# A softmax's row sums in the spare columns of the score bank

## The chip, the core and the metric

The kernel runs on one core of a Trainium2 chip. The core has a matrix engine (TensorE, in the profile PE, with its weight loads as PEld), a vector engine (VectorE, DVE), an engine for functions (ScalarE, ACT), a general engine (GpSimd, POOL) and one that issues transfers (SyncE, SP). Each works through its own queue in order, and they wait for one another by semaphores. TensorE writes into PSUM, a small memory of eight banks with 512 fp32 columns on each of 128 partitions; SBUF is the large working memory. The metric is the time of one execution on the device, in microseconds.

## The reference

Three stages follow one another: sparse attention over 2 batches of 8 heads, 576 positions, 64 values a head; then four experts, each token weighting all of them; then a gated layer. What the change touches is the attention's softmax:

```
scores = scale * q @ k.T
mask_local   = (rel >= 0) & (rel < 32)                 # heads 0 to 3
mask_strided = (rel >= 0) & (pos_k % 32 == pos_q % 32) # heads 4 to 7
scores = where(mask, scores, -1e9)
scores = scores - max(scores, axis=-1)
attn = exp(scores)
attn = attn / (sum(attn, axis=-1) + 1e-09)
out = attn @ v
```

The result is turned to tokens by features and goes through the experts (`relu(x @ w1) @ w2`, weighted) and the gated layer (`sigmoid(x @ wg) * (x @ wv) @ wo`).

## The kernel before

The order of every engine's instructions is written out in the program; no scheduler changes it. A ledger in the program adds up assumed costs and decides from them where background work (conversion of weights) is put between the steps of the later stages.

The attention is cut into 32 groups, 16 in each batch. A group of the strided kind is a score tile of 72 rows by 4 blocks of 72 columns (288 columns), one of the local kind 96 rows by 3 blocks of 128 (384 columns); in each batch eight strided groups come first, then eight local ones. The first batch runs by itself at the start of the program (with small matmuls of zeros, `keep_warm`, in TensorE's pauses), the second is interleaved with the first products of the first expert. `attention` is a software pipeline: in step i the stages of `STAGES` run in the order values, transpose, scores, exp, norm, split, each on the group that it has come to:

- `pair_scores`, every other step, for two groups: two masks are written into two PSUM banks (line 717, tile `sps`), then the products of queries and keys are added to them (line 730). The pool of these banks has three of them; a bank is given to the next group when the instructions that used it are over.
- `group_exp`, for group i: VectorE takes the negated maximum of each block (`nm<-sps`), then ScalarE takes one exponential for each block (`P<-sps,nm`), with the maximum as bias. Each has an accumulator output: the sum over the block goes to one column of a small SBUF tile, `sm`. In the profile that output is a row of its own, ACTIVATION_READ_ACCUMULATOR, behind each ACTIVATE.
- `group_norm`, one step later: VectorE adds 1e-9 to the sums (TENSOR_SCALAR `sm<-sm`), takes the reciprocal, and GpSimd multiplies the exponentials by it in place (`P<-P,sm`).
- `group_transpose`, three steps behind: TensorE transposes the blocks into another bank (`tps`, line 756), VectorE copies them out (`PT`).
- `group_values`, `group_split`, five steps behind: the product with the values (line 780), and its split into a high and a low part (`xh`, `xl`) for the experts.

Around the groups the queries and keys are transposed by TensorE (`qkps`) and copied by ScalarE (`qsT`, `qlT`) and VectorE (`ksT`, `klT`), one pair of groups or more ahead; GpSimd and ScalarE split the weights of the first expert (`wh`, `wl`); the first expert's hidden values are evacuated by ScalarE (`hh`) and VectorE (`hl`). Helpers record these calls, so that all instructions of the three engines have line 101 in the profile, and tiles tell them apart.

Of the kernel before, what the change touches and what calls it, by code (L numbers as in the profile page):

```python
# [9 lines left out]
F32 = mybir.dt.float32  # L10
# [6 lines left out]
AF = mybir.ActivationFunctionType  # L17
ALU = mybir.AluOpType
# [88 lines left out]
def attn_moe_glu_kernel(ctx, tc, q, k, v, dp, w1, w2, wg, wv, wo, out):  # L107
    nc = tc.nc
    ledger = Ledger()
    dve, act, pool_ = (Reckoned(e_, name, ledger) for e_, name in ((nc.vector, "V"), (nc.scalar, "A"), (nc.gpsimd, "G")))  # L110
# [26 lines left out]
    atp = at_stack.enter_context(tc.tile_pool(name="atp", bufs=1, side="right", reuse_waits="tile"))  # L137
# [527 lines left out]
    pt_tiles, of_tiles, soft = {}, {}, {}  # L665
# [42 lines left out]
    def pair_scores(pair):  # L708


        tiles = []
        for kind, b, c, half, hh in pair:
            ps = sp_.tile([128, 512], F32, tag="s", name="sps")
            n, w, m = (NU, NU, 4) if kind == "s" else (96, 128, 3)
            pv_ = ps[:n, :m * w].rearrange("p (a b) -> p a b", b=w)
            mask = mask_s.unsqueeze(1).to_broadcast([NU, 4, NU]) if kind == "s" else mask_l[:, half:half + 3, :]
            nc.tensor.matmul(pv_, identb[:n, :n], mask, start=True, stop=False)  # L717
            soft[kind, b, c, half, hh] = (pv_, n, w, m)
            tiles.append(pv_)
        m = soft[pair[0]][3]  # L720
        for j in range(m):
            for pv_, (kind, b, c, half, hh) in zip(tiles, pair):
                if kind == "s":
                    lo = 64 * half
                    qs_, ks_ = QT["s", b, c, hh][lo:lo + 64, j, :], KT["s", b, c, hh][lo:lo + 64, j, :]
                else:
                    lo, i = 64 * c, 3 * half + j
                    q0, k0 = hh * S + 96 * i, hh * S + max(96 * i - 32, 0)
                    qs_, ks_ = QT["l", b][lo:lo + 64, q0:q0 + 96], KT["l", b][lo:lo + 64, k0:k0 + 128]
                nc.tensor.matmul(pv_[:, j, :], qs_, ks_, start=False, stop=j == m - 1)  # L730

    def group_exp(g):
        pv_, n, w, m = soft[g]
        nm = atp.tile([128, 4], F32, tag="nm", name="nm", bufs=4)
        sm = atp.tile([128, 4], F32, tag="sm", name="sm", bufs=4)
        pt = atp.tile([128, 384], F32, tag="P", name="P", bufs=3)
        pp = pt[:n, :m * w].rearrange("p (a b) -> p a b", b=w)
        dve.tensor_reduce(nm[:n, :m], pv_, AX.X, ALU.max, negate=True)
        for j in range(m):
            act.activation(  # L740
                pp[:, j, :], pv_[:, j, :], AF.Exp, bias=nm[:n, j:j + 1], accum_out=sm[:n, j:j + 1]
            )
        soft[g] = (pp, sm[:n, :m], n, w, m)

    def group_norm(g):
        pp, sm, n, w, m = soft[g]
        dve.tensor_scalar(sm, sm, 1e-9, None, ALU.add)
        dve.reciprocal(sm, sm)
        pool_.tensor_tensor(pp, pp, sm.unsqueeze(2).to_broadcast([n, m, w]), ALU.mult)

# [63 lines left out]
    def attention():  # L814

        gs = []
        for b in range(B):
            gs += [("s", b, c, half, hh) for c in range(2) for hh in range(2) for half in range(2)]
            gs += [("l", b, c, half, hh) for half in range(2) for hh in range(2) for c in range(2)]
        n = len(gs)  # L820
        stage = dict(values=group_values, transpose=group_transpose, scores=pair_scores,
                     exp=group_exp, norm=group_norm, split=group_split)

        def later(x):
# [564 lines left out]
```

## Time and profile before

| | us |
|---|---|
| median of the runs shown | 651.19 |
| lowest of them | 650.22 |
| the profiled execution | 651.06 |
| its span, first to last instruction | 648.9 |
| TensorE busy | 638.2 (98%) |
| VectorE busy | 440.3 (68%) |
| ScalarE busy | 341.7 (53%) |
| GpSimd busy | 265.5 (41%) |

The span is the profile's own; the 2.2 us between it and the execution's time lie ahead of the first and behind the last instruction. Times in a trace are counted from the start of the span. A busy TensorE is not one at its peak, since matmuls are pipelined and their ends are modelled. Idle time of an engine that nobody waits for costs nothing.

### The profile page before, as it was taken

What the parts mean: (1) busy time and instruction counts of PE and PEld (TensorE: products, weight loads), DVE (VectorE), ACT (ScalarE), POOL (GpSimd) and SP (SyncE); (2) the same over time, 40 slices, a digit from 0 to 9 for tenths busy, and PEclk for the clock granted to TensorE, in tenths of its full rate; (3) what the DMA queues carried; (4) which work ended last, traced back from release to release, by engine and by line L of the source; (5) the groups of instructions that cost most, each with busy time, mean ns of one, the idle gap of its engine ahead of it and who ended that gap; (6) DMA issues with size and microseconds to landing.
All of it is one profiled execution on the core that took longest, in us unless ns stands there. A gap on an engine that the chain in (4) does not pass through costs nothing.

```text
span 648.9 us, 12702 instructions
## 1 busy us (share of the span) xinstructions
PE 638.2 (98%) x4899; PEld 469.3 (72%) x4904; DVE 440.3 (68%) x885; ACT 341.7 (53%) x807; POOL 265.5 (41%) x307
## 2 busy tenths in 40 slices
PE   8889999999999999999999999999999999999998
PEld 5668889999676666666666666666979877987794
DVE  4876586787461886693887788898866659633432
ACT  5747553554854646774645554642565574532230
POOL 3665561000422226361335335440465377453540
PEclk9999999999999999999999999999999999999999
DMA  9965141030421544251664464354113832330002
GB/s 184 243 172 141 35 117 43 1 115 17 142 86 57 158 147 159 81 182 59 183 255 143 163 227 147 98 162 146 35 34 117 286 142 81 107 132 1 33 19 97
DMA packets 48884, 77.00 MB, mean 119 GB/s; under 512 B 19540, under 2 KB 24440, under 8 KB 47672
## 3 DMA queue, kind: packets, MB, share of 16 engines
q1 hardware_dynamic: 48824, 76.20, 37.6%
q8 instruction: 38, 0.62, 0.4%
q14 instruction: 22, 0.18, 0.1%
HBM read 59.66 MB, written 16.53 MB: 117 GB/s over the span
## 4 chain that ended last, share of the span: by engine, by line
PE 94%; DVE 1%; DMA 1%; SPq 1%; ACT 1%; issue 0%; POOL 0%; POOLq 0%; ACTq 0%
PE gps L874 23%; PE gps L876 23%; PE gps L875 23%; PE gps L976 19%; SPq L173 1%; PE sps L730 1%; PE warm L264 1%; PE tps L756 1%; PE o L780 1%; DMA ks<-in_k_dram 1%; ACT P L101 1%; DMA kl<-in_k_dram 1%; PE qkps L698 0%; PE qkps L676 0%; PE sps L717 0%; DVE nm L101 0%
## 5 line engine op out<-in xcount | busy, mean ns | idle before, releaser
L101 POOL TENSOR_TENSOR hl<-t,hh 128x384 f16<-128x384 f32 x72 | 76.5, 1065 | 179.2 <-ACT t L101 175.4
L976 PEld LDWEIGHTS <-w 128*128 128x128 f16 x1512 | 125.0, 98 | 1.8
L976 PE MATMUL gps<-x,w 128*128 128x192 f16 x1512 | 126.2, 246 | 0.0
L874 PE MATMUL gps<-x,w 128*128 128x384 f16 x288 | 93.9, 326 | 0.0
L875 PE MATMUL gps<-x,w 128*128 128x384 f16 x288 | 93.9, 326 | 0.0
L876 PE MATMUL gps<-x,w 128*128 128x384 f16 x288 | 93.9, 326 | 0.0
L874 PE MATMUL gps<-hh,w 128*128 128x384 f16 x288 | 93.9, 326 | 0.0
L875 PE MATMUL gps<-hl,w 128*128 128x384 f16 x288 | 93.9, 326 | 0.0
L876 PE MATMUL gps<-hh,w 128*128 128x384 f16 x288 | 93.9, 326 | 0.0
L874 PEld LDWEIGHTS <-w 128*128 128x128 f16 x576 | 56.4, 98 | 37.3 <-issue 0.2
L876 PEld LDWEIGHTS <-w 128*128 128x128 f16 x576 | 56.4, 98 | 37.2
L875 PEld LDWEIGHTS <-w 128*128 128x128 f16 x576 | 56.4, 98 | 36.4
L101 ACT ACTIVATE hh<-gps 128x384 f16<-128x384 f32 (+1 forms) x96 | 46.8, 487 | 48.8 <-PE gps L876 48.5
L101 POOL TENSOR_TENSOR stage<-magn,stage 128x512 f16<-128x512 f32 x36 | 45.5, 1273 | 45.1 <-ACT magn L101 38.9
L101 ACT ACTIVATE w<-raw,up 128x512 f16<-128x512 f32 x48 | 32.0, 715 | 34.8 <-DVE up L101 34.7
L101 ACT ACTIVATE P<-sps,nm 72x72 f32<-72x72 f32 (+1 forms) x112 | 36.4, 333 | 23.8 <-DVE sm L101 17.0
L101 ACT ACTIVATE bits<-raw 128x512 f32<-128x512 f32 x36 | 24.3, 674 | 38.1 <-DVE magn L101 37.9
L101 DVE SCALAR_TENSOR_TENSOR w<-raw,up,w 128x512 f16<-128x512 f32 x48 | 40.1, 871 | 5.1 <-ACT w L101 4.9
L101 POOL TENSOR_TENSOR sg<-four,sg 128x384 f32<-128x384 f32 x9 | 9.6, 1069 | 80.8 <-DVE four L101 77.9
L874 PE MATMUL gps<-w,hh 128*128 128x512 f16 (+1 forms) x112 | 41.6, 371 | 0.0
L875 PE MATMUL gps<-w,hh 128*128 128x512 f16 (+1 forms) x112 | 41.6, 371 | 0.0
L876 PE MATMUL gps<-w,hl 128*128 128x512 f16 (+1 forms) x112 | 41.6, 371 | 0.0
(145 smaller groups left out, 1281.5 us busy)
## 6 DMA issues: line engine op xcount, KB each, us to landing
raw<-in_moe_w_dram SPq DMA_DIRECT2D x32, 512.0 KB
raw<-in_moe_w_gate_dram SPq DMA_DIRECT2D x12, 512.0 KB
raw<-in_moe_w_val_dram SPq DMA_DIRECT2D x12, 512.0 KB
raw<-in_moe_w_out_dram SPq DMA_DIRECT2D x12, 512.0 KB
wg<-stage SPq DMA_DIRECT2D x21, 256.0 KB
wv<-stage SPq DMA_DIRECT2D x21, 256.0 KB
w<-wg SPq DMA_DIRECT2D x3, 1024.0 KB
wo<-stage SPq DMA_DIRECT2D x12, 256.0 KB
```

The lines of the kernel that those rows point to most:

```text
L101: return f(*a, **k)
L173: nc.sync.dma_start(t[:, :, j, :], src[b, 2 * j:2 * j + 2].rearrange("h s d -> (h s) d").rearrange("(c p) d -> p c d", p=128),)
L264: nc.tensor.matmul(ps, zero.to_broadcast([128, 128]), zero.to_broadcast([128, 512]), start=True, stop=True,)
L730: nc.tensor.matmul(pv_[:, j, :], qs_, ks_, start=False, stop=j == m - 1)
L756: nc.tensor.transpose(pv_[:, j, :], pp[:, j, :], ident[:n, :n])
L780: nc.tensor.matmul(o[x * 64:x * 64 + 64, j * n:(j + 1) * n], lhsT, tts[x][:, j, :], start=True, stop=True)
L874: nc.tensor.matmul(ps, ah, bh, start=first and i == 0, stop=False)
L875: nc.tensor.matmul(ps, ah, bl, start=False, stop=False)
L876: nc.tensor.matmul(ps, al, bh, start=False, stop=last and i == n - 1)
L976: nc.tensor.matmul(o, l_, r_, start=first and x + kk + y == 0, stop=last and x * kk * y == 2, skip_group_check=True)
```

## The change

`pair_scores` keeps, beside the view of a group's scores, a view of the last columns of the same bank: the last 4 of 512 for a strided group, the last 3 for a local one. `group_exp` gives these columns to the exponentials as their accumulator output in place of the SBUF tile. `group_norm` allocates the SBUF tile and writes the sum plus 1e-9 into it, reading PSUM; the reciprocal is as before. No instruction is added or taken away, and none changes its place.

```diff
@@ pair_scores
-            soft[kind, b, c, half, hh] = (pv_, n, w, m)
+            soft[kind, b, c, half, hh] = (pv_, ps[:n, 512 - m:], n, w, m)
             tiles.append(pv_)
-        m = soft[pair[0]][3]
+        m = soft[pair[0]][4]
@@ group_exp
-        pv_, n, w, m = soft[g]
+        pv_, sums, n, w, m = soft[g]
         nm = atp.tile([128, 4], F32, tag="nm", name="nm", bufs=4)
-        sm = atp.tile([128, 4], F32, tag="sm", name="sm", bufs=4)
...
-                pp[:, j, :], pv_[:, j, :], AF.Exp, bias=nm[:n, j:j + 1], accum_out=sm[:n, j:j + 1]
+                pp[:, j, :], pv_[:, j, :], AF.Exp, bias=nm[:n, j:j + 1], accum_out=sums[:, j:j + 1]
             )
-        soft[g] = (pp, sm[:n, :m], n, w, m)
+        soft[g] = (pp, sums, n, w, m)
@@ group_norm
-        pp, sm, n, w, m = soft[g]
-        dve.tensor_scalar(sm, sm, 1e-9, None, ALU.add)
+        pp, sums, n, w, m = soft[g]
+        sm = atp.tile([128, 4], F32, tag="sm", name="sm", bufs=4)[:n, :m]
+        dve.tensor_scalar(sm, sums, 1e-9, None, ALU.add)
         dve.reciprocal(sm, sm)
```

What the change does to the waits shows in two places. The first is ScalarE's queue at the fourth and fifth group of the first batch. In a row, the tiles left of the arrow are written and those right of it read, the bracket names the engines whose semaphores the instruction waits for (Activation is ScalarE itself), and x3 stands for three such rows. Before:

```order
L101 ACTIVATE qsT<-qkps 128x288 [waits PE_49]
L101 ACTIVATE P,sm<-sps,nm 72x72 [waits DVE_49,PE_49,Pool_49]
L101 ACTIVATE P,sm<-sps,nm 72x72 x3
L101 ACTIVATE qsT<-qkps 128x288 [waits PE_49]
L101 ACTIVATE P,sm<-sps,nm 72x72 [waits DVE_49,Pool_49]
```

And in the changed kernel, at the same place:

```order
L101 ACTIVATE qsT<-qkps 128x288 [waits PE_49]
L101 ACTIVATE P,sps<-sps,nm 72x72 [waits DVE_49,PE_49,Pool_49]
L101 ACTIVATE P,sps<-sps,nm 72x72 [waits Activation_49] x3
L101 ACTIVATE qsT<-qkps 128x288 [waits PE_49]
L101 ACTIVATE P,sps<-sps,nm 72x72 [waits DVE_49,Pool_49]
```

The second to fourth exponential of a group waited for nothing and now wait for the one before them.

The second place is TensorE's queue at the second pair of the first batch, where the fourth group takes the bank of the first (`ms` is the strided mask, `identb` the identity that it is multiplied by; a minus is the kernel before, a plus the changed one):

```order
 L717 LDWEIGHTS identb
 L717 MATMUL sps<-ms,identb 72x288
-L717 LDWEIGHTS identb [waits DVE_49]
-L717 MATMUL sps<-ms,identb 72x288 [waits Activation_49]
-L730 MATMUL sps<-ksT,qsT 72x72 [waits DVE_49,Activation_49]
+L717 LDWEIGHTS identb
+L717 MATMUL sps<-ms,identb 72x288 [waits DVE_49]
+L730 MATMUL sps<-ksT,qsT 72x72 [waits Activation_49]
 L730 MATMUL sps<-ksT,qsT 72x72 x7
```

The mask of the fourth group waited for ScalarE, the last exponential of the first group; it now waits for VectorE, the first group's addition.

## Rows read from the trace of the kernel before

**Rows 1.** Engines by stretch: us, busy PE, PEld, DVE, ACT, POOL; PE clock, DMA, GB/s.

```profile
5.00:20.00 15.00, 14.01 (x172) 10.28 (x174) 9.55 (x33) 11.13 (x64) 3.98 (x6) 1.00 1.13 210
20.00:47.00 27.00, 22.37 (x256) 17.07 (x257) 22.61 (x69) 16.25 (x70) 19.73 (x23) 1.00 0.83 212
47.00:55.45 8.45, 7.87 (x73) 7.03 (x69) 4.07 (x14) 5.55 (x29) 2.61 (x3) 1.00 0.93 237
55.45:104.00 48.55, 47.97 (x431) 41.78 (x432) 34.80 (x90) 25.81 (x113) 28.26 (x36) 1.00 0.25 74
104.00:648.00 544.00, 541.75 (x3970) 391.67 (x3968) 368.78 (x680) 281.64 (x533) 207.56 (x225) 1.00 0.34 114
```

**Rows 2.** Instructions on the score banks: duration in ns, least, median and longest.

```profile
L101 ACT ACTIVATION_READ_ACCUMULATOR P<-sps,nm x112: 187/195/222, 8.2 to 93.5; 72x1 f32 x64, 96x1 f32 x48
L101 DVE TENSOR_REDUCE nm<-sps x32: 442/498/554, 7.5 to 91.9; 72x4 f32<-72x288 f32 x16, 96x3 f32<-96x384 f32 x16
```

**Rows 3.** ScalarE in order of time, inside the first group: start and duration, us.

```profile
8.18 0.19 ACT L101 ACTIVATION_READ_ACCUMULATOR P<-sps,nm 72x1 f32 x1
8.27 0.30 ACT L101 ACTIVATE P<-sps,nm 72x72 f32<-72x72 f32 x1
```

**Rows 4.** ScalarE in order of time, two magnitude passes over an expert's weights.

```profile
120.19 0.19 ACT L101 ACTIVATION_READ_ACCUMULATOR junk<-raw 128x1 f32 x1
120.42 1.06 ACT L101 ACTIVATE junk<-raw 128x1024 bf16<-128x1024 f32 x1
```

**Rows 5.** VectorE's groups by form: busy us, mean ns, idle time before them.

```profile
L101 DVE TENSOR_SCALAR sm<-sm 96x3 f32<-96x3 f32 x16 | 6.1, 380 | 0.6 <-ACT of L101 0.4 <-POOL P L101 0.3
...
L101 DVE TENSOR_SCALAR sm<-sm 72x4 f32<-72x4 f32 x16 | 3.9, 245 | 0.8 <-ACT P L101 0.8
...
L101 DVE DVE_READ_ACCUMULATOR bits<-bits 128x1 f32 x36 | 3.0, 82 | 0.0
```

**Rows 6.** Engines by stretch, from the first exponential to a copy of queries.

```profile
7.96:24.42 16.46, 15.86 (x194) 11.63 (x195) 12.72 (x44) 14.62 (x83) 6.99 (x11) 1.00 1.09 203
```

**Rows 7.** TensorE's weight loads in order of time, scores of the sixth pair.

```profile
24.95 0.25 PEld L730 LDWEIGHTS sps<-klT,qlT 64*96 64x96 f32 x4 [0.56 <-ACT qlT L101]
```

**Rows 8.** The chain that ended last, 47 to 56 us: start, us, what.

```profile
47.81 1.31 ACT P L101 x8
...
51.06 1.31 ACT P L101 x8
...
55.10 0.31 ACT qsT L101
...
55.45 0.44 PE gps L874
```

**Rows 9.** Instructions on the sums' tile: ns least, median, longest; first and last start.

```profile
L101 DVE TENSOR_SCALAR sm<-sm x32: 153/158/1208, 9.3 to 93.8; 72x4 f32<-72x4 f32 x16, 96x3 f32<-96x3 f32 x16
```

**Rows 10.** All engines in order of time, the last group of the first batch.

```profile
36.29 1.28 POOL L101 TENSOR_TENSOR wl<-raw,wh 128x512 fp32r<-128x512 f32 x1
36.52 1.07 DVE L101 TENSOR_SCALAR sm<-sm 96x3 f32<-96x3 f32 x1
...
38.85 0.39 PE L756 MATMUL tps<-ident,P 96*128 96x96 f32 x2 [0.42 <-POOL P L101]
```

**Rows 11.** VectorE in order of time, two places.

```profile
12.18 0.44 DVE L101 TENSOR_REDUCE nm<-sps 72x4 f32<-72x288 f32 x1
12.54 0.15 DVE L101 TENSOR_SCALAR sm<-sm 72x4 f32<-72x4 f32 x1
...
54.25 0.44 DVE L101 COPY PT<-tps 72x288 f32<-72x288 f32 x1
...
54.61 0.44 DVE L101 TENSOR_REDUCE nm<-sps 72x4 f32<-72x288 f32 x1
```

**Rows 12.** All engines in order of time, hidden values of the first expert.

```profile
57.83 0.56 DVE L101 SCALAR_TENSOR_TENSOR hl<-gps,hh 128x384 fp32r<-128x384 f32 x1 [1.90 <-ACT hh L101]
...
58.69 0.33 PE L875 MATMUL gps<-hl,wh 128*128 128x384 f32 x1
```

## The prediction

> **What bounds the kernel now.** I read the busy time of each engine by stretch first, then the chain of work that ended last, and only then single instructions; the busy share of the whole span, 98% for TensorE, hides where the holes are. From 104 us on TensorE stands still for 2.3 of 544 us, and from 55.45 to 104 us for 0.6 of 48.6 us; it stands still for 1.0 us between 5 and 20, 4.6 us between 20 and 47 and 0.6 us between 47 and 55.45 [rows 1]. All 32 softmax groups lie before 95 us [rows 9]. So a change to them can move the end only where TensorE is late because of them: in the first batch (5 to 38 us), where scores, exponentials, sums and transposes follow each other around a loop, and in the start of the second (47 to 55.45 us). There the chain of waits runs through ScalarE's exponentials for three groups in a row before it returns to TensorE at 55.45 us [rows 8]. Behind 55.45 TensorE has work queued, and the other engines have to be late by more than their slack to matter. In the order of instructions nothing has moved; what differs is buffers and waits. A shift at 55.45 us therefore goes to the end unshortened.
>
> **The added waits on ScalarE.** Each exponential is followed by a row that writes out its sum, 112 of them, median 195 ns [rows 2]. Before, the next exponential starts 0.09 us after that row starts, while it still runs [rows 3]. In the changed order all but the first exponential of a group carry a wait on ScalarE itself, since each now reads the bank into which the one before writes its sum: 3 in each of 16 strided groups, 2 in each of 16 local ones, 80 in all. The trace shows this pattern elsewhere: the magnitude passes at 119 us carry the same wait behind the same kind of row, and there the next one starts 0.23 us after it (120.19 to 120.42) [rows 4]. So one wait costs 0.23 - 0.09 = **0.14 us**: 0.42 us for a strided group, 0.28 for a local one, and 16 x 0.42 + 16 x 0.28 = 11.2 us of ScalarE time.
>
> The row of the sum that is written into PSUM is in no trace here. Bounds: the longest of the 112 rows is 222 ns [rows 2], which makes a wait 0.17 us; VectorE's row of the same kind takes 82 ns [rows 5], which makes it 0.03. No end lies below nothing, since the wait only delays. I take 0.14, from the row of the same engine.
>
> The Trainium skill, "ScalarE: Activation LUTs", Step-by-step, says that ScalarE writes PSUM sooner than SBUF, and "Perfetto Trace Analysis", Optimizing Scalar/DVE Operations, gives some 51 ns against 93 of access; by that estimate a wait costs 0.10 us, and the whole sum below would be about +1.4 us. No run here shows it yet.
>
> **What of it is on the path, first batch.** By 24.42 us, where the transposed queries of the next pair go to SBUF, ten exponential groups have run: 8 x 0.42 + 2 x 0.28 = 3.92 us more. TensorE waits for exactly that copy (24.95, its weight loads idle for 0.56 us) [rows 7]. In 7.96 to 24.42 ScalarE is busy 14.62 of 16.46 us [rows 6], so 1.84 us can be absorbed, and 2.1 us can't. When one of its pauses closes, the next exponential also starts 0.09 us inside the one before; over the three pauses that close, that gives back 0.3. I take **+1.8 us** at 24.95. From there on each local group has 0.28 us more, but ScalarE is busy only 16.25 of the 27 us to 47 [rows 1], so it is no longer last, and the shift is carried round the loop without growing.
>
> **What is removed.** The addition now reads PSUM. Before, its 32 rows have a median of 158 ns and a longest of 1208 [rows 9]. The longer ones lie under a GpSimd instruction: at 36.52 the addition takes 1.07 us, until GpSimd's subtraction (36.29, 1.28 us) is over [rows 10]. They hold 4.9 us in all: 32 rows at 158 ns are 5.1 us, and the two groups by form sum to 10.0 [rows 5]. The reductions that read PSUM have a longest row of 554 ns for 384 elements, under the same GpSimd traffic [rows 2], so I expect every addition to take 0.15 to 0.17 us. On the path is only the one at 36.52: the transposes at 38.85 wait 0.42 us for GpSimd's multiplication behind it [rows 10]. That can't start before 37.57, where the subtraction ends, and with the sums of the last group later by 0.28 us for itself the gain shrinks to **-0.2 us** (bounds 0 and -0.4). The other long rows lie behind 60 us, where TensorE has its own queue to work off, and a short one at the start of the local half ends before GpSimd is free: nothing.
>
> That the addition reads PSUM costs nothing that the rows show: the distance from a 288-element row to the next is 0.36 us whether the next reads SBUF (12.18 to 12.54) or PSUM (54.25 to 54.61) [rows 11]. I bound it at 0.02 us. The Trainium skill, "Perfetto Trace Analysis", same section, speaks against the change here, with 125 ns of VectorE access on PSUM against 60 on SBUF; by it each of the eight pairs of the first batch would lose 0.07, and the sum would be 0.5 us higher. The equal distances don't bear that out.
>
> **Second batch, 47 to 55.45.** Three strided groups stand in series with the copies and subtractions behind them (exponentials at 47.81, at 51.06 and once more before the copy of the queries at 55.10, TensorE at 55.45) [rows 8]. Nothing on ScalarE covers them: the weights' conversion and the evacuation of the first expert stand in the same queue behind the exponentials. 3 x 0.42 = **+1.26 us**. Behind 55.45 one place has too little slack: the low half of the hidden values is ready at 58.39 and TensorE takes it at 58.69 [rows 12]; with 0.05 us of signalling the slack is 0.25, the fourth group delays it by 0.42: **+0.17 us**. After that TensorE has 3.3 us of its own matmuls for each group, and ScalarE from 55.45 to 104 is busy 25.8 of 48.6 us [rows 1]: it absorbs the rest.
>
> **The bank that is held longer.** A score bank was free when its exponentials had read it; now it is free when the addition has. Three banks serve pairs, so the second mask matmul of a pair waits for the addition of the group three back. On VectorE that addition stands right behind a reduction that is over by then, so it follows the last exponential by one row of 0.16 us and its signalling, some 0.2 us. Queued behind the waiting mask matmul are the pair's scores, and for those the reductions. In the strided half of the first batch ScalarE delays the pair anyway, and in the rest the addition is long over; it is within the 1.8.
>
> **Sum.** 1.8 - 0.2 + 1.26 + 0.17 = +3.0 us. The profiled execution took 651.06 us with a span of 648.9; the median of the runs shown is 651.19, 0.13 off. So **654.1 us**, 0.5% slower. About 2% (13 us) is what a measurement of this kernel tells from no change.
>
> **Rivals.**
> (a) The wait is nearly free, and the stalls decide: *not slower*. If the sum's row into PSUM ends as soon as the 82 ns row, a wait costs 0.03 us; 28 of them by 24.42 are 0.84 us, which ScalarE's 1.84 us of pauses swallow but for some 0.1; the second batch pays 9 x 0.03 = 0.27; the stall gives back up to 0.4. Sum 0.0, and with no wait at all -0.4: 650.7 to 651.1 us. For it: the exponentials' next start doesn't hang on their output row now. Against: the wait hangs on that row's end, and all ScalarE rows of the kind take 187 to 222 ns [rows 2]. It decides below 0.05 us a wait. Halfway, with rows of some 155 ns, a wait costs 0.10 us, and the sum is (2.8 - 2.1) + 0.9 - 0.2 = +1.4: 652.5 us. The skill's rule on ScalarE and PSUM is this halfway case.
> (b) The held bank becomes the loop's last link. If mask matmuls wait for the addition in all seven later pairs of the first batch, 7 x 0.2 = 1.4 us come on top: 655.5 us. For it: the order shows the new wait at every pair from the second on. Against: ScalarE's pauses behind 20 us leave the addition time.
> (c) TensorE's clock falls. All stretches have 1.00 granted, the 2.4 GHz level [rows 1], 20 to 47 us among them with 17% idle. The change takes 5 to 20 us from 7% idle to about as much. If 47 to 55.45 ran at the 1.2 GHz level, its 7.9 us of matmuls would take 7.9 more, and 5 to 20 us as much as 14: 662 to 668 us, slower by up to 2.6%. Against: the idler stretch kept its clock.
>
> **Chances.** Forecast (653 to 655 us) 0.55; (a), with the halfway case, 0.24; (b) 0.15; (c) 0.04; 0.02 for a gain that I don't see. The range takes in (a) down to 650.9; above, waits of 0.17 us make the same sum (28 x 0.17 - 2.14) + 9 x 0.17 + 0.26 - 0.2 = +4.2 us, 655.3, and (b) on top of that 656.7, of which I leave out the last: 650.9 to 656.5. Faster by over 2% 0.01, within 2% 0.95, slower by over 2% 0.04: only (c) reaches it.
>
> **What will show it.** Right, if a group's exponentials start 0.43 us apart instead of 0.30, no addition takes over 0.3 us, TensorE idles some 2 us more before 38 us and some 1.3 more between 47 and 57, and the stretch behind keeps its length. Wrong, if the distance is under 0.35 (then (a)), if mask matmuls wait on VectorE for more than 0.2 us (b), or if a granted clock is under 1.00 (c). It would also be wrong if the loads that stand in SyncE's queue behind the first batch ended the waits up to 44 us; then part of the 1.8 us is hidden.

## The result, and the profile after

| | before | after |
|---|---|---|
| median of five runs each, us | 651.09 | 654.92 |
| lowest to highest of after, us | | 653.63 to 656.48 |
| ratio, 95% interval | | 1.0061 [1.005, 1.0072] |
| the profiled execution, its span, us | 651.06, 648.9 | 654.94, 652.8 |

The changed kernel takes 3.8 us more, 3.3 to 4.7 by the interval of the ratio. The highest of its five runs had a mean granted clock of 0.992, the others 0.999 or 1.0. One of the five runs of before took 1335.52 us, twice the others, for a reason that isn't on record; the ratio goes by the others.

The page's busy times of the changed kernel come first: ScalarE has 4.7 us more than in the table of before, VectorE 4.7 us less.

```profile
PE 639.9 (98%) x4899; PEld 469.6 (72%) x4904; DVE 435.6 (67%) x885; ACT 346.4 (53%) x807; POOL 265.3 (41%) x307
```

The rows on the score banks of the changed kernel (duration in ns: least, median, longest) answer to [rows 2] and [rows 9].

```profile
L101 ACT ACTIVATION_READ_ACCUMULATOR P<-sps,nm x112: 154/156/169, 8.7 to 97.7; 72x1 f32 x64, 96x1 f32 x48
...
L101 DVE TENSOR_SCALAR sm<-sps x32: 146/148/158, 10.1 to 97.9; 72x4 f32<-72x4 f32 x16, 96x3 f32<-96x3 f32 x16
```

The row that writes a sum is 39 ns shorter into PSUM (156 for 195). No addition is long any more, the longest is 158 ns for 1208. ScalarE in order of time, inside the first group, answers to [rows 3]:

```profile
8.46 0.32 ACT L101 ACTIVATE P<-sps,nm 72x72 f32<-72x72 f32 x1 [1.91 <-DVE nm L101]
8.68 0.16 ACT L101 ACTIVATION_READ_ACCUMULATOR P<-sps,nm 72x1 f32 x1
8.87 0.32 ACT L101 ACTIVATE P<-sps,nm 72x72 f32<-72x72 f32 x1
```

The next exponential now starts 0.19 us after the row of the sum (8.68 to 8.87), where it was 0.09. It waits for the row's end and 0.03 us more, as the magnitude passes do behind their longer row [rows 4]. A wait costs 0.10 us, and the exponentials of a strided group follow each other after 0.41 us, where it was 0.30; in a local group it is 0.45 for 0.35.

TensorE's waits of the changed kernel between 5 and 110 us (us in total, times, the longest):

```profile
PE tps L756 <- POOL P L101: 2.3, 4, 0.7
PE sps L717 <- DVE sm L101: 1.4, 4, 0.7
...
PE sps L730 <- ACT qlT L101: 0.7, 1, 0.7
...
PE gps L874 <- ACT hh L101: 0.2, 1, 0.2
...
PE gps L875 <- DVE hl L101: 0.2, 1, 0.2
```

The second line is the held bank: four masks wait for an addition, one of them 0.7 us; no mask (L717) waits for VectorE in the kernel before. The last two are new as well; they lie at 95 us. The last group of the first batch, all engines in order of time, answers to [rows 10]:

```profile
38.69 1.27 POOL L101 TENSOR_TENSOR wl<-raw,wh 128x512 fp32r<-128x512 f32 x1
...
39.11 0.16 DVE L101 TENSOR_SCALAR sm<-sps 96x3 f32<-96x3 f32 x1 [0.18 <-ACT P L101]
...
39.92 0.82 POOL L101 TENSOR_TENSOR P<-P,sm 96x384 f32<-96x384 f32 x1
...
40.80 0.47 PE L756 MATMUL tps<-ident,P 96*128 96x96 f32 x3
```

GpSimd's multiplication follows its subtraction at once (38.69 + 1.27 = 39.96). Before, the reciprocal stood behind the stalled addition, and the multiplication came 0.40 us after the subtraction's end (36.29 + 1.28 = 37.57):

```profile
37.97 0.82 POOL L101 TENSOR_TENSOR P<-P,sm 96x384 f32<-96x384 f32 x1 [0.40 <-DMA kl<-in_k_dram]
```

(The bracket names a transfer, but the instruction that ended just ahead is the reciprocal, 37.63 to 37.80.) In the changed kernel, the chain that ended last, 49 to 58.5 us, answers to [rows 8]:

```profile
49.75 0.38 ACT P L101 x2
...
50.98 0.38 ACT P L101 x2
...
53.30 0.38 ACT P L101 x2
...
56.34 0.38 ACT P L101 x2
...
57.94 0.34 ACT qsT L101
58.32 0.45 PE gps L874
```

The same three groups and the same copy; from 46.49 to 55.45 it took 8.96 us, now from 48.43 to 58.32 9.89.

**Where the time went.** All instructions stand in the same order in both kernels, so a matmul of before can be found in the trace after and their starts subtracted. For 38.85 us that is 40.80 - 38.85 = 1.95. The start of a run moves by itself: the first scores began at 6.73 before and at 7.23 after, and in the kernels below from 0.87 us earlier to 0.50 later, though nothing ahead of them differs (what moves it stands at the end of the section on why the prediction was right). I take that difference off each trace's shifts: 1.95 - 0.50 = 1.45. In kernels that share a stretch the shifts so counted agree within a few hundredths of a us. This is the table on which the rest stands; its columns are times in the trace of before (a transpose, a transpose, scores, a product of the expert and so on), its entries TensorE's delay there in us.

| kernel | 16.23 | 24.95 | 36.88 | 38.85 | 46.49 | 55.45 | 60.38 | 80.0 | 92.0 | end |
|---|---|---|---|---|---|---|---|---|---|---|
| changed | 0.85 | 1.22 | 1.89 | 1.45 | 1.44 | 2.37 | 2.53 | 2.46 | 3.40 | 3.38 |
| e1 waits | 0.50 | 1.71 | 1.58 | 1.59 | 1.57 | 2.50 | 2.68 | 2.68 | 3.59 | 3.57 |
| e11 waits, again | 0.73 | 1.34 | 1.78 | 1.79 | 1.78 | 2.70 | 5.77 | 5.72 | 6.65 | 6.63 |
| e2 bank | 0.74 | 0.75 | 0.86 | 0.42 | 0.42 | 0.68 | 0.64 | 0.77 | 0.79 | 0.78 |
| e12 bank, again | 0.25 | 0.26 | 0.40 | -0.04 | -0.03 | 0.24 | 0.19 | 0.17 | 0.18 | 0.17 |
| e4 batch 1 | 0.85 | 1.23 | 1.90 | 1.47 | 1.44 | 1.43 | 1.42 | 1.38 | 1.42 | 1.40 |
| e9 batch 1, local | 0.01 | 0.55 | 1.24 | 0.80 | 0.78 | 0.78 | 0.78 | 0.76 | 0.77 | 0.76 |
| e6 strided | 0.85 | 0.86 | 0.82 | 0.83 | 0.81 | 1.74 | 1.90 | 1.86 | 1.90 | 1.88 |
| e5 batch 2, local | 0.00 | 0.00 | -0.02 | -0.01 | -0.01 | -0.02 | -0.03 | -0.05 | 0.86 | 0.85 |
| e7 no addition, PSUM | 0.89 | 1.26 | 1.16 | 0.72 | 0.70 | 1.63 | 1.78 | 1.44 | 2.36 | 2.35 |
| e3 no addition | -0.13 | -0.12 | -0.74 | -1.18 | 0.30 | 0.32 | 0.30 | -0.06 | -0.05 | -0.06 |
| e8 the same, warm | -0.13 | -0.12 | -0.74 | -1.19 | -1.21 | -1.22 | -1.24 | -1.61 | -1.61 | -1.61 |
| e10 warm alone | 0.00 | 0.01 | -0.01 | 0.00 | 0.00 | 0.00 | 0.01 | 0.02 | 0.02 | 0.02 |

So the changed kernel loses 1.89 us in the first batch, gets 0.44 back at its last group, loses 0.93 at the start of the second, 0.16 at 60 us, and 0.9 more between 80 and 92 us, where the prediction had nothing. That makes 3.38; the profiled execution is 3.88 above that of before because it also began 0.50 later.

### The profile page after: what moved, and what is told of

The parts are those of the page before. It is cut to its first block, busy times and chain, and to the rows that moved or that the text cites. A ratio compares the mean times of both kernels' runs of the same rounds, so it can differ in the third digit from the quotient of the medians.

```text
span 652.8 us, 12698 instructions
## 1 busy us (share of the span) xinstructions
PE 639.9 (98%) x4899; PEld 469.6 (72%) x4904; DVE 435.6 (67%) x885; ACT 346.4 (53%) x807; POOL 265.3 (41%) x307
## 4 chain that ended last, share of the span: by engine, by line
PE 92%; ACT 4%; DVE 3%; issue 1%; DVEq 0%; ACTq 0%
PE gps L874 23%; PE gps L875 22%; PE gps L876 22%; PE gps L976 19%; ACT P L101 3%; PE sps L730 1%; PE warm L264 1%; PE tps L756 1%; PE o L780 1%; DVE nm L101 1%; PE qkps L698 1%; DVE hl L101 1%; DVE sm L101 0%; PE sps L717 0%; PE qkps L676 0%
```

## The experiments

Theory 1 was that the waits on ScalarE carry the loss, theory 2 that the bank which is held until the addition carries it. Medians stand beside those of the kernel before on the same chip. The order of instructions on every engine is that of before in all of them, but for an instruction left out, exchanged or added as told.

**e1 and e11, the waits alone.** The diffs are against the changed kernel, e1 first:

```diff
-        soft[g] = (pp, sums, n, w, m)
+        soft[g] = (pp, nm[:n, :m], n, w, m)
```

> The sums go into the score bank as in the changed kernel, so every exponential but a group's first still waits for the one before; but the addition reads the negated maxima in SBUF, so nothing on VectorE reads the bank and it is free after its last exponential. (The softmax is then divided by the wrong number.) Theory 1, the waits on ScalarE carry the loss: exponentials 0.41 us apart in a strided group and 0.45 in a local one as in the changed kernel, no mask matmul waiting for VectorE, +2.5 to +3.5 us against the kernel before (ratio 1.0038 to 1.0054). Theory 2, the bank held until the addition carries it: +0.5 to +1.5 us (ratio 1.0008 to 1.0023).

```diff
-        dve.tensor_scalar(sm, sums, 1e-9, None, ALU.add)
+        dve.tensor_scalar(sm, pp[:, :, 0], 1e-9, None, ALU.add)
```

> The waits on ScalarE alone, once more: the sums go into the score bank, the addition reads the first column of each block of exponentials in SBUF (so the softmax is divided by the wrong number), which keeps VectorE's wait for the last exponential and its SBUF operands as before; nothing but the exponentials keeps the bank. In the first such run a late transfer of the values, 0.8 us, fell into the first batch and hid what belongs to the waits there. Theory: waits +0.5 us by 16.2 us of before's count and +1.2 to +1.7 by 36.9, the stalled addition still there (none of the -0.44), second batch +0.9, +0.16, +0.85 as in the changed kernel: +3.1 to +3.6 us in the trace (ratio 1.0044 to 1.006). Rival, the held bank is needed for the first batch's loss: under +0.8 us by 36.9, +2.7 us or less.

Measured: e1 653.6 us for 651.14, ratio 1.0053 [1.0037, 1.0069]; no mask waits for VectorE. But its first batch is not clean, as TensorE's waits in e1 between 6.6 and 39 us show:

```profile
PE tps L756 <- POOL P L101: 2.4, 4, 0.7
PE o L780 <- DMA vs<-in_v_dram: 0.8, 1, 0.8
```

This run began 0.87 us early, and the values had not landed. e11 has the waits with only 0.2 us of that: 1.78 us by 36.88, +0.92 at the second batch's start, +0.86 between 80 and 92. Between 55.45 and 60.38 it lost 3.07 us where the changed kernel loses 0.16, and the engines by stretch tell why (the last columns are TensorE's granted clock, the DMA share and GB/s):

```profile
54.00:57.50 3.50, 2.15 (x18) 1.51 (x17) 2.68 (x10) 2.36 (x11) 0.66 (x1) 1.00 0.51 169
58.00:59.00 1.00, 1.00 (x8) 0.86 (x7) 0.00 (x0) 0.90 (x6) 1.00 (x1) 0.64 0.00 0
59.00:64.00 5.00, 5.00 (x31) 4.30 (x30) 2.18 (x6) 2.96 (x13) 2.63 (x4) 0.50 0.00 0
```

TensorE stood still for 1.35 of 3.5 us, and then ran at half its clock, the 1.2 GHz level, from 58.3 until 65.1 us. Why it did, these rows don't settle: e1 has the same pauses and kept its clock.

```profile
54.00:57.50 3.50, 2.15 (x17) 1.52 (x16) 2.86 (x10) 2.36 (x12) 0.66 (x1) 1.00 0.46 176
59.00:64.00 5.00, 5.00 (x48) 4.36 (x48) 4.10 (x11) 3.88 (x19) 2.62 (x4) 1.00 0.00 0
```

Four of e11's six runs have a mean clock of 0.989 to 0.995, which makes its ratio 1.0083 [1.0064, 1.0102], above the expected range; the two at 1.000 took 654.31 and 654.36 us, 3.6 above 650.74. So the waits alone cost 3.6 to 3.7 us (6.63 less 3.07, plus 0.16), without the stall's gain. e1, whose profiled run kept its clock, ends at 3.57 in the table, with the same +0.93, +0.18 and +0.91 in the second batch. Theory 1 holds.

**e2 and e12, the bank alone.** Sums in SBUF as before; `sp` is the view of spare columns of the bank in e2, and of the first column of each block of scores in e12; e2 first:

```diff
-        dve.tensor_scalar(sm, sm, 1e-9, None, ALU.add)
-        dve.reciprocal(sm, sm)
+        dve.tensor_scalar(sp, sm, 1e-9, None, ALU.add)
+        dve.reciprocal(sm, sp)
```

> The sums go into SBUF as in the kernel before; the addition reads them there and writes into the spare columns of the score bank, and the reciprocal reads these. No exponential waits for the one before; the bank is held until the reciprocal, some 0.17 us longer than in the changed kernel. Theory 1: exponentials 0.30 us apart, mask matmuls wait for VectorE but ScalarE has the time; 0 to +0.6 us (ratio 1.0000 to 1.0009). Theory 2: +2 to +3.5 us (ratio 1.003 to 1.0054). Both: the addition has an operand in PSUM, so no addition takes over 0.3 us.

```diff
-        dve.tensor_scalar(sm, sm, 1e-9, None, ALU.add)
+        dve.scalar_tensor_tensor(sm, sp, 0.0, sm, ALU.mult, ALU.add)
```

> The held bank alone, as long as in the changed kernel: sums in SBUF, no wait on ScalarE; in place of the addition of 1e-9 (which changes no sum of at least 1) VectorE adds to the sums a column of the score bank times zero, so the bank is held until that instruction, and not until the reciprocal as in the earlier run. Theory: +0.3 to +0.6 us by 16.2 us, +0.4 to +0.7 by 36.9, -0.44 for the stall, +0.1 to +0.3 at the second batch's start, nothing behind: +0.2 to +0.7 us in the trace (ratio 1.0002 to 1.0011). Rival, ScalarE has the time for it as the prediction said: 0 to +0.2 by 36.9 and -0.4 to -0.2 at the end (ratio 0.9993 to 0.9998).

Measured: e2 651.71 us for 651.14, ratio 1.0011 [1.0002, 1.0019]; e12 651.3 us for 650.74, 1.0008 [0.9999, 1.0017]. e12's row on the sums and its one long wait of a mask, TensorE in order of time:

```profile
L101 DVE SCALAR_TENSOR_TENSOR sm<-sps,sm x32: 145/147/158, 9.0 to 93.7; 72x4 f32<-72x4 f32 x16, 96x3 f32<-96x3 f32 x16
```

```profile
50.76 0.32 PE L717 MATMUL sps<-ms,identb 72*72 72x288 bf16 x1 [0.39 <-DVE sm L101]
```

Held until the addition, the bank costs 0.40 us by 36.88 and 0.27 at the second batch; held 0.17 us longer, 0.86 and 0.26. That is between the two theories when it stands alone; in e12 the 0.25 by 16.23 and the 0.17 at the end lie just under what I expected, and the interval of its ratio includes 1. Beside the waits it adds nearly nothing: 1.89 in the changed kernel against 1.78 in e11 by 36.88, 0.93 against 0.92 in the second batch. The two delays lie side by side. In both kernels the -0.44 is there.

**e3, e7, e8 and e10, the addition left out.** A sum of exponentials from which the maximum was taken is at least 1, so the addition can go. e3 is the kernel before without the line (a line for the ledger stands in its place, so that the background work stays where it was); e7 is the changed kernel so, and its reciprocal reads `sums`. e8 is e3 with more matmuls of zeros, e10 the kernel before with these alone:

```diff
-        dve.tensor_scalar(sm, sm, 1e-9, None, ALU.add)
+        ledger.add("V", "tensor_scalar", {}, (sm,))
...
-EMPTY = {0: 2, 1: 4, 2: 2, 3: 2, 4: 2, **{i: 2 for i in range(5, 16, 2)}, 16: 1, 19: 1, 20: 1}
+EMPTY = {0: 2, 1: 4, 2: 2, 3: 2, 4: 2, **{i: 2 for i in range(5, 16, 2)}, 16: 1, 19: 5, 20: 1}
```

> The kernel before without the addition of 1e-9 (a sum of exponentials is at least 1, so it leaves the fp32 sum as it is); the reciprocal reads the sums in SBUF. No wait, no held bank, no stalled addition. If the stall at 36.52 was worth what the prediction said: -0.2 to -0.4 us, and another -0.1 to -0.3 from 0.17 us less between sums and reciprocal in each group of the first batch: -0.3 to -0.7 us (ratio 0.9989 to 0.9995). Rival: the reciprocal, now the first to read the sums, stalls under GpSimd in the addition's place, with rows of over 0.5 us: ratio 0.9995 to 1.0005.

> The changed kernel without the addition: the reciprocal reads the sums in the score bank. Waits on ScalarE stay, the bank is held 0.16 us less. Theory, the waits alone carry the loss and the addition's place on the chain is a cost of its own: 0.17 us less in each pair of the first batch and what the kernel without addition gained behind it, 1.0 to 1.3 us less than the changed kernel: +2.2 to +2.8 us against before (ratio 1.0034 to 1.0043). Rival, the held bank carries part of it: over 1.5 us less than the changed kernel (ratio under 1.0032).

> The kernel without the addition, sums in SBUF, with five instead of one matmul of zeros at step 19, in TensorE's pause of 1.3 us before the transposed weights of the tokens at 42 us. The profiled run of the kernel without them had the 1.2 GHz level from 44 to 47 us and lost 1.5 us there; two more of its twelve runs... were near its time. If idling there is what lowers the clock: mean clock 0.999 or 1.0 in all runs, none above 650.5 us, median 649.0 to 649.7 (ratio 0.9970 to 0.9980). Rival: the clock falls as often, or the added matmuls delay TensorE by up to 0.8 us: ratio 0.998 to 0.9995.

> The kernel before with five instead of one matmul of zeros at step 19 and nothing else. If all that they do is keep the clock, which the kernel before holds in nearly all of its runs: ratio 0.9993 to 1.0003, and the gain of the kernel without addition and with these matmuls, 1.6 us in the trace, is that of the missing addition. Rival: they are worth something by themselves: ratio under 0.9988.

Measured: e3 649.51 us for 651.14, ratio 0.9982 [0.9974, 0.9991]; e7 653.47 for 650.97, 1.0042 [1.003, 1.0055]; e8 649.1 for 650.97, 0.9973 [0.9964, 0.9982]; e10 650.81 for 650.86, 0.9996 [0.9987, 1.0004]. The reciprocal that takes over the reading of the sums in SBUF doesn't stall; e3's row:

```profile
L101 DVE RECIPROCAL sm<-sm x32: 159/164/174, 9.8 to 94.2; 72x4 f32<-72x4 f32 x16, 96x3 f32<-96x3 f32 x16
```

e3 gains 1.18 us by 38.85, more than the 0.3 to 0.7 that I had expected. Of this 0.74 stand there before the place of the stall: the loop has 0.17 us less between sums and reciprocal, and TensorE waits for GpSimd's multiplications 1.4 us in e8 up to 39 us, 2.8 before. The other 0.44 is the stall. Another 0.37 comes between 60 and 80 us and makes e8's 1.61; there TensorE's wait for the transposed keys falls from 0.6 to 0.4 us, and the rest I haven't traced. It isn't the stalls, since the changed kernel has none either and gains 0.07 there. e7 is 1.03 us better than the changed kernel, which is the addition's place on the chain once more and leaves nothing for the rival.

The profiled run of e3 lost 1.5 us between 38.85 and 46.49. Its engines by stretch, and TensorE in order of time:

```profile
43.00:44.00 1.00, 0.71 (x12) 0.58 (x7) 0.93 (x6) 0.00 (x0) 0.46 (x1) 0.97 1.01 381
44.00:47.00 3.00, 3.00 (x12) 2.69 (x10) 1.22 (x4) 1.11 (x2) 1.27 (x1) 0.50 0.17 61
```

```profile
42.43 0.27 PE L298 MATMUL pps<-ident,ptok 128*36 128x128 f32 x1 [1.27 <-DVE ptok L101]
...
44.09 0.52 PE L875 MATMUL gps<-xl,wh 128*128 128x384 f32 x1
```

A pause of 1.27 us, and behind it the 1.2 GHz level for 3.4 us (44.0 to 47.4), with the expert's matmuls at 0.52 us, 0.34 elsewhere. Filled with four matmuls of zeros (e8), the same place:

```profile
43.00:44.00 1.00, 0.70 (x6) 0.69 (x5) 0.97 (x5) 0.62 (x1) 0.19 (x1) 1.00 0.63 238
44.00:47.00 3.00, 3.00 (x31) 2.65 (x30) 1.41 (x4) 0.69 (x2) 1.29 (x1) 1.00 0.19 52
```

All of e8's eleven runs have a mean clock of 0.999 or 1.0, and the highest took 649.79 us; e3 had two of twelve at 0.996 and 0.997 (the expectation of e8 counts one too many). None of eleven against two of twelve, on two different chips, doesn't show that the four matmuls hold the clock. The kernel before has the same pause, and keeps its clock behind it in nearly all runs; there the four matmuls are worth nothing (e10). e8 is faster than both kernels, by 0.27% than the one before.

**e4, e5, e6 and e9, the change in some groups only.** The changed kernel, where a condition decides between the bank's columns and an SBUF tile. `COND` is `g[1] == 0` in e4, `g[:2] == ("l", 1)` in e5, `g[0] == "s"` in e6 and `g[:2] == ("l", 0)` in e9:

```diff
+        if not (COND):
+            sums = atp.tile([128, 4], F32, tag="sm", name="sm", bufs=4)[:n, :m]
...
-        sm = atp.tile([128, 4], F32, tag="sm", name="sm", bufs=4)[:n, :m]
+        if COND:
+            sm = atp.tile([128, 4], F32, tag="sm", name="sm", bufs=4)[:n, :m]
+        else:
+            sm = sums
```

> The change in the first batch's 16 groups only; the second batch keeps its sums in SBUF. By the trace of the changed kernel the first batch is 1.4 us later at the second's start beyond the 0.5 us that its first loads came later: +1.2 to +2.0 us (ratio 1.0018 to 1.0031), and the second batch as long as before. Rival: the 0.5 us at the start belongs to the change: +1.9 to +2.3 us. Rival 2: the shift of the first batch is swallowed where the second meets it: under +0.8 us.

> The change in the second batch's eight local groups only. In the changed kernel's trace TensorE becomes 0.85 us later at 92 to 93 us (of before's count), behind those groups. Theory: their exponentials, the evacuation behind them on ScalarE, the low half behind it on VectorE and the next reduction behind that wait for each other in a circle, so 0.18 us a group adds up although ScalarE idles; nothing moves up to 80 us, then +0.7 to +0.9 us (ratio 1.0010 to 1.0014). Rival, as the prediction had it: ScalarE's idle time takes it up, and the 0.85 us is a late effect of the earlier shift: 0 to +0.2 us (ratio 1.0000 to 1.0003).

> The change in the 16 strided groups of both batches; local groups keep their sums in SBUF. Theory: most of the first batch's loss (+1.7 to +2.0 us by 38 us, with the stalled addition at 36.5 still there), +0.93 at the start of the second batch, +0.16 at 61 us, nothing at 93: +2.7 to +3.1 us (ratio 1.0041 to 1.0048), only 0.3 to 0.7 us less than the whole change. Rival: local groups carry a large part of the first batch's loss: under +2.2 us (ratio under 1.0034).

> The change in the first batch's eight local groups only. With the strided groups alone the first batch lost 0.83 us by 36.5 us (of before's count), with all its groups 1.9 and, behind the addition that no longer stalls, 1.45. Theory: the local groups lose on their own, since the transposes wait for GpSimd behind their exponentials in each pair although ScalarE idles in 40% of that time: +0.8 to +1.1 us by 36.5 us, -0.44 there, +0.4 to +0.7 us at the end (ratio 1.0006 to 1.0011). Rival, as the prediction had it: ScalarE's pauses take the local groups' waits up and only the strided groups' delay is carried through: 0 to +0.2 by 36.5, -0.4 to -0.2 at the end (ratio 0.9994 to 0.9997).

Measured: e4 652.71 us for 651.14, ratio 1.0027 [1.0018, 1.0035]; e5 652.15 for 650.97, 1.0019 [1.001, 1.0028]; e6 652.52 for 650.97, 1.0032 [1.0019, 1.0044]; e9 651.75 for 650.86, 1.0019 [1.001, 1.0028]. e4 is the changed kernel up to 46.49 and loses nothing behind it; it also began 0.73 us early, so the 0.50 of the changed kernel's start isn't the change's. In e6 my expectation failed and its rival held: the strided groups cost the first batch only 0.82 us. The local ones, alone in e9, cost it 1.24 by 36.88, more than I had expected, and -0.44 behind.

The ratios of e4 and e9 lie above the table, if within their intervals (0.27% and 0.19% against 1.40 and 0.76 us, or 0.22% and 0.12%). Three runs of each had a mean clock of 0.997. Counted over all kernels here that have the new waits in the first batch's local groups together with the addition (changed, e1, e4, e9, e11), 13 of 40 runs had 0.997 or less; of the kernel before it was 1 in 89. So such falls came far more often in these kernels, and the ratios contain them where the table, apart from the rows of e3 and e11, doesn't. e3 had falls without the waits, and e7 has the waits and no fall in its five runs, on another chip: which pause brings the fall isn't shown.

e5 moves nothing up to 80 us and then 0.86. How, the changed kernel's local groups at the same place show, all engines in order of time:

```profile
91.24 0.49 ACT L101 ACTIVATE hh<-gps 128x384 fp32r<-128x384 f32 x1
91.76 0.56 DVE L101 SCALAR_TENSOR_TENSOR hl<-gps,hh 128x384 fp32r<-128x384 f32 x1 [1.45 <-ACT hh L101]
...
92.60 0.55 DVE L101 TENSOR_REDUCE nm<-sps 96x3 f32<-96x384 f32 x1
...
93.24 0.36 ACT L101 ACTIVATE P<-sps,nm 96x128 f32<-96x128 f32 x1 [1.51 <-DVE sm L101]
...
94.46 0.51 ACT L101 ACTIVATE hh<-gps 128x384 fp32r<-128x384 f32 x1
...
95.01 0.56 DVE L101 SCALAR_TENSOR_TENSOR hl<-gps,hh 128x384 fp32r<-128x384 f32 x1 [1.59 <-ACT hh L101]
95.03 0.44 PE L874 MATMUL gps<-hh,wh 128*128 128x384 f32 x1 [0.21 <-ACT hh L101]
...
95.62 0.44 PE L875 MATMUL gps<-hl,wh 128*128 128x384 f32 x1 [0.15 <-DVE hl L101]
```

Read the brackets: VectorE waits for `hh`, ScalarE's exponentials wait for VectorE, and the next `hh` stands behind these exponentials. Each engine is idle for 1.5 us in this turn, and neither has any time to spare, because each idles for the other. The two waits of a local group add 0.2 us to a turn: the groups' first exponentials, at 77.47, 81.02, 84.58, 85.97 and 89.52 before, are later by 3.00, 3.18, 3.36, 3.53 and 3.72 us by the bare difference of starts. (The first local groups, at 70.73 and 73.89, are later by 3.00 too: there the idle time still took the waits up.) Then the hidden values come too late for TensorE, which had 0.19 us in hand at the low half before (ready at 91.64, taken at 91.83):

```profile
91.08 0.56 DVE L101 SCALAR_TENSOR_TENSOR hl<-gps,hh 128x384 fp32r<-128x384 f32 x1 [0.32 <-ACT hh L101]
...
91.83 0.34 PE L875 MATMUL gps<-hl,wh 128*128 128x384 f32 x1
```

## Why the prediction was right, by its steps

The forecast was 654.1 us and the time 654.92, within its range; the sum of 3.0 us stands against 3.38 in the trace. It was right with the help of errors that cancel: 1.8 - 0.2 + 1.26 + 0.17 were forecast, 1.89 - 0.44 + 0.93 + 0.16 + 0.85 measured, and the 1.89 are not the ones that were meant. By the price that a wait really had, 0.10 us, the prediction's own sum is the halfway case of its rival (a), +1.4 us. What it let idle time absorb was too much by 1.2 us in the first batch and by 0.16 and 0.85 behind 55.45, 2.2 us in all; the price, too high by 0.04 a wait, hid most of that.

- **The wait, 0.14 us.** Too large: the row into PSUM takes 156 ns, near the halfway case of rival (a), whose price of 0.10 us is what was measured. On this the Trainium skill, "Perfetto Trace Analysis", Optimizing Scalar/DVE Operations, agrees with the trace: it has 51 ns of access on PSUM for 93 on SBUF, the row is 39 ns shorter. The sign that I had named, 0.43 us between exponentials, came out as 0.41; a strided group takes 0.32 us more, not 0.42.
- **First batch, +1.8 at 24.95, and nothing behind.** The failed step. There stand 1.22 us, and 1.89 only at 36.88. The step took ScalarE's idle time, 1.84 us up to 24.42 and 40% of what follows, for room that takes the waits up. e6 and e9 split it: 0.82 from the strided groups, to which 3.36 of the 3.92 us behind the 1.8 belonged, and some 1.1 from the local groups, for which the prediction had nothing, "so it is no longer last". As I read the waits, ScalarE idles there for reductions, and these wait for scores, transposes and GpSimd's multiplications behind its own exponentials; that two kinds of groups lose is measured, the path between them no run tests by itself. That the sum came out near 1.8 is a coincidence of two errors.
- **The stall, -0.2.** It gave 0.44 us (e4, e9, e12, e3 alike, and nothing in e11, whose addition has all its operands in SBUF and whose GpSimd idles 0.40 us there as before). I took off 0.2 for the last group's later sums; but those had time until GpSimd's subtraction ended, so all of the 0.40 between it and the multiplication came back.
- **The addition reads PSUM, 0.02 or less.** Right: 148 ns for a median of 158 from SBUF. The 0.07 us per pair that the prediction worked out from the Trainium skill, "Perfetto Trace Analysis", Optimizing Scalar/DVE Operations, shows in no row: from a local group's reduction to the addition behind it it is 0.47 us with the sums in PSUM (92.60 to 93.07) as with the sums in SBUF (91.92 to 92.39 before); the rows decide.
- **Second batch, +1.26 and +0.17.** The path was right, the size went with the wait: three groups at 0.32 are 0.96, measured 0.93; the low half of the hidden values 0.16.
- **"ScalarE absorbs the rest" behind 55.45.** Wrong by 0.85 us, shown by e5; the same mistake as in the first batch, between ScalarE and VectorE.
- **The bank, within the 1.8.** Right in what it costs (0.1 us beside the waits). But the sign that I had named for rival (b), masks that wait over 0.2 us for VectorE, did appear, 1.4 us in four waits, and cost next to nothing: e11 has none of these waits and is as late. A wait that is new isn't yet a delay.
- **The clock (c).** It held in the profiled run. One of the five runs, at 0.992, was 1.6 us above the median, and e3 and e11 show what such a fall is worth: 1.5 and 3 us, since it ends after 3 to 7 us. My 8 us and more for a whole stretch was too large. Whether it was the cause in that run of the changed kernel stays open; its trace wasn't kept.

What moves the start of a run by up to 1.4 us, the traces tell. The program begins with eleven matmuls of zeros, here in e11 and in the changed kernel, with the transposes behind them:

```profile
0.78 3.96 PE L264 MATMUL warm<-const-float32-0.0 128*128 128x512 bf16 x11 [0.78 <-PEq L1374]
4.57 0.41 PE L676 MATMUL qkps<-ident,qs 72*128 72x72 f32 x4
```

```profile
0.78 4.85 PE L264 MATMUL warm<-const-float32-0.0 128*128 128x512 bf16 x11 [0.78 <-PEq L1374]
5.43 0.68 PE L676 MATMUL qkps<-ident,qs 72*128 72x72 f32 x4
```

In e11 these matmuls start 0.43 us apart at first and 0.22 apart from 3.70 us on, so TensorE came to twice its speed there; in the changed kernel it is slow through all eleven and through the transposes. Each trace's first record of the clock, at 1.00, begins at that change: 3.62 us in e1, 3.67 in e11, 5.41 before, 6.60 in the changed kernel, and the first scores follow in the same order in all fourteen traces (5.86, 5.88, 6.73 and 7.23 in these four). Ahead of that record the views print 1.00 though nothing was recorded. So the start moves with the time at which TensorE came to the 2.4 GHz level, and not with the change.

## What to carry to other kernels

Before you let an engine's idle time absorb a new delay, follow what ends each idle stretch: if it leads back to the same engine's own output, the idle time is part of a loop, and its length doesn't tell how much it can absorb. An accumulator output into the bank that the next instruction reads makes a chain of instructions out of a pipeline; it cost 0.1 us for each of 80 exponentials, and 3.6 of these 8 us came out at the end. And where a small instruction stalls, ask first if it is needed: leaving out the addition took away the same stall, shortened the loop besides, and made the kernel 0.18% faster (e3, with a fallen clock in two of its runs; 0.27% in e8, with none), where the change made it 0.6% slower.

## What the runs showed of the hardware

- VectorE's addition with one operand in PSUM, read (changed kernel, e12) or written (e2), had no row over 161 ns in 32, where the addition with both operands in SBUF had rows of up to 1208 (before) and 1519 ns (e1). The reciprocal on the same tile in SBUF had none over 176 ns in any run, also where it came first (174 in e3).
- TensorE's clock fell to the 1.2 GHz level for 3.4 us (e3) and 6.8 us (e11) behind a pause of 1.27 us and behind three shorter ones (1.35 us idle in 3.5). It didn't fall in the profiled run of the kernel before, which has the same pause, 1.26 us, up to 43.15, nor in that of e1, which has both. Ten of e3's twelve runs, the same program, have a mean clock of 0.999 or 1.0.
- Once the first scores had started, traces of kernels that share a stretch repeated each other to some 0.03 us. Against single runs that scatter by more than 1 us (650.1 to 651.9 in 88 of 89 of the kernel before), the shift of one matmul is the finer measure.
